# The zeros of an accumulated output: 24 small DMAs in the first stage, or one large DMA behind weight loads

## The chip, the core and the metric

The kernel runs on one core of one Trainium2 chip. The metric is the device time of one execution in microseconds (us). The matrix engine is PE (its weight loads PEld), the vector engine DVE, the scalar engine ACT, GpSimd POOL, and SP is the engine that does nothing but issue DMAs and wait. SP, ACT and POOL each put DMAs into a queue of their own (q1, q10 and q0 in the profile); 16 DMA engines work on all queues.

## The reference

Three layers follow one another on 3072 tokens (4 batches of 768) of 512 values (8 heads of 64):

```
state = gamma * state + k[t] v[t]^T ;  y[t] = scale * q[t] state        # retention, per batch and head
logits = x @ phi ; d = softmax over tokens ; c = softmax over slots     # soft MoE: 8 experts x 4 slots
slots = d.T @ x ; slot_out[e] = relu(slots[e] @ w1[e]) @ w2[e] ; x = c @ slot_out
logits = x @ w_gate + log1p(exp(x @ w_noise)) * noise                   # second MoE: top 2 of 8 experts
out[mask] += weight * (relu(x[mask] @ w1[e]) @ w2[e])                   # for each expert e
```

The last line sums into an output that starts as zeros, and this is where the zeros of this case come from.

## The kernel before

All inputs and the output are float32. The work has three stages, in one program.

*Retention and logits* (lines 203 to 468). A loop over `j` takes 24 chunks of 128 tokens, one ahead in some steps. PE transposes k (`k_t`) and q (`q_t`), multiplies them (`qk`), and forms the output (`y_out`) and the state (`kv`); `x_n` turns the output back. DVE scales the transposed q into `qT` (L267), masks the products into `am` (L287) and scales the result into `xT` (L308). ACT and POOL prepare k and v. For every four chunks, the functions `group0` to `group4` do the softmax of the soft MoE step by step. On SP the loop also issues the loads of q, k and v, and the first MoE's first weights W1 in 28 parts (L456). And it writes the zeros: at L457 to L461, in chunks 1 to 21, DVE makes a zero tile `zt` of 128 x 128 (the bits of `xT`, and-ed with 0, so that it runs no earlier than that chunk) and SP sends it to the output, repeated four times along a row, 256 KB a DMA in pieces of 512 bytes. The tile has two buffers, so that DVE waits before the third for the first one's DMA.

*First MoE's experts and the gate* (lines 469 to 644). `ph` (L516) multiplies the slots with W1, `po` (L549) with W2. W2's parts are loaded by SP into buffers as these come free (`load_w`, L187). At L565 to L567 SP then loads the second MoE's first weights: V1[0], V2[0] and V1[1], 2 MB each, V1[1] into the pool `ringv`. Next come the gate logits, the choice of two experts (DVE, `top`, `cand`, `sel`) and the weights `wsl`. At L639 ACT's queue writes `wsl` into the table `ctab` in memory, two DMAs in which each value row is 8 numbers, 32 bytes, and behind them come three of the four parts of V1[2] (L644).

*Second MoE's experts* (from L647). `lists` finds for each expert the tokens that chose it. `fetch` gathers their rows of `ctab` (L748), so that it needs the writes of L639. `turn` splits and transposes them into `cts`; `hidden` (L801) multiplies with `gs`, the slot outputs already multiplied with V1; `main` (L834 to L836) multiplies with V2, each float32 product as three. `add_rows` (L815) adds the rows to the output in memory, by an indirect DMA of POOL. Before the first expert, ACT casts V2[0] into its high parts (`wh`, L776), splits `g` (L665) and copies it (L681), all in order.

What sets the order around the change: each engine runs its instructions in the order of the program as scheduled, and each waits for its own inputs. SP's order behind the weights of the first experts is: V1[0], V2[0], V1[1], then the copies of `gs` for expert 1 (L687).

Of the kernel before, what the change touches and what calls it, by code (L numbers as in the profile page):

```python
# [9 lines left out]
F32 = mybir.dt.float32  # L10
F32R = mybir.dt.float32r
F16 = mybir.dt.float16
I32 = mybir.dt.int32
AF = mybir.ActivationFunctionType
OP = mybir.AluOpType
# [4 lines left out]
N = B * S  # L20
DM = H * D
P = 128
C = 128
NC = S // C
NCH = B * NC
HP = H // 2
# [10 lines left out]
TL = 64  # L37
LB = SB + 1
WP = 19
ZP = 21  # L40
HV = 7
FB, FN = 7, 6
F1, F2, F3, F4 = 2, 0, 0, 26
# [60 lines left out]
def kernel(ctx: ExitStack, tc: tile.TileContext, q, k, v, phi, w1, w2,  # L104
                              wg, wn, noise, v1, v2, csta, cst, cst16, out):
    nc = tc.nc
# [24 lines left out]
    def after(*ins):  # L131
        stack = ExitStack()
        for i in ins:
            stack.enter_context(tc.issue_after(i.ins if hasattr(i, "ins") else i))
        return stack

    def fill(pool, tag, n, bufs=None):
        if not n:
            return
        pw = pool.tile([P, DM], F32, name="pw", tag=tag, bufs=bufs)  # L140
        for i in range(n):
            nc.tensor.matmul(pw, ones, ones[:, None, :].to_broadcast([P, 4, P]), start=True, stop=True)
# [44 lines left out]
    def load_w(store, src, e, eng, ring, halves=False):  # L187
        t = ring.tile([P, 4096], F32, name="w", tag="w")
        if store is V2:
            nc.sync.dma_start(t.rearrange("p (k n) -> p k n", k=KF), src[e].rearrange("(k p) n -> p k n", p=P))  # L190
            store[e] = t
            return
        s = src[e].rearrange("(p k) n -> p (k n)", p=P)
        if halves:
            tv, sv = (a.rearrange("p (g i n) -> p i g n", g=4, i=2) for a in (t, s))
            for i in range(2):
                eng.dma_start(tv[:, i], sv[:, i])
        else:
            eng.dma_start(t, s)
        store[e] = t  # L200
# [3 lines left out]
    with ExitStack() as actx:  # L204
        work = actx.enter_context(tc.tile_pool(name="work", bufs=2))
        small = actx.enter_context(tc.tile_pool(name="small", bufs=2))
# [6 lines left out]
        def load_q(t):  # L213
            b, u = divmod(t, NC // 2)
            x = comp[:, t % 2]
            nc.sync.dma_start(
                x.rearrange("p h r d -> p h (r d)"),
                q[b, :, 256 * u:256 * u + 256, :].rearrange("h (p r) d -> p h (r d)", r=2))
            QL[t] = x
# [7 lines left out]
        def load_kv(u, gs=range(2)):  # L227
            b, t = divmod(u, NC // 2)
            raw = RAW.setdefault(u, [])
            for i, src in enumerate(() if raw else (k, v)):  # L230
                x = raws[:, 2 * (u % 2) + i]
                nc.sync.dma_start(x.rearrange("p h r d -> p h (r d)"),
                                  src[b, :, 256 * t:256 * t + 256, :].rearrange("h (p r) d -> p h (r d)", r=2))
                raw.append(x)
            for g in gs:
                j = 2 * u + g
                if u % 2:
                    KL[j] = io.tile([P, H, D], F32, name="kl", bufs=2)
                    VL[j] = io.tile([P, H, D], F32, name="vl", bufs=2)
                else:  # L240
                    KL[j], VL[j] = (comp[:, 2 + i].rearrange("p h r d -> p (h r d)")[:, DM * g:DM * g + DM]
                                    .rearrange("p (h d) -> p h d", h=H) for i in range(2))
                gs = slice(64 * g, 64 * g + 64)
                for r in range(2):
                    rs = slice(64 * r, 64 * r + 64)
                    nc.scalar.copy(KL[j][rs], raw[0][gs, :, r, :])
                    pool_ins[0] = nc.gpsimd.tensor_tensor(VL[j][rs], raw[1][gs, :, r, :],  # L247
                                            gv[gs, r, t, :, None].to_broadcast([64, H, D]), op=OP.mult)
# [21 lines left out]
        def k_t(j):  # L270
            pt = psA.tile([P, HP, P], F32, name="pt", tag="pt")
            for hp in range(HP):
                nc.tensor.transpose(pt[:, hp, :], KL[j][:, 2 * hp:2 * hp + 2, :], ident)
            KT[j] = io.tile([P, HP, P], F32, name="kT", bufs=2)
            return nc.scalar.copy(KT[j], pt)  # L275

        def qk(j):
            t, g = divmod(j, 2)
            pa = [psA.tile([P, HP, P], F32, name="pa", tag="pa") for _ in range(2)]
            for hp in range(HP):  # L280
                for s in range(2):
                    r = slice(64 * s, 64 * s + 64)
                    mm = nc.tensor.matmul(pa[s][:, hp, :], KT[j][r, hp, :], QT[t][r, hp, g, :],  # L283
                                          start=True, stop=True)
            for s in range(2):
                a = io.tile([P, HP, P], F32, name="am", bufs=3)
                nc.vector.tensor_tensor(a, pa[s], mask_b, op=OP.mult)  # L287
                AM[j, s] = a
            return mm

        pS = psA.tile([P, HP, D], F32, name="pS", bufs=1)
        X, XT = {}, {}
# [106 lines left out]
            nc.vector.tensor_copy(cT[:, g, :], pc)  # L399

        NT = NCH // 2
        ov = out.rearrange("(p a) d -> p a d", p=P)
        fill(psA, "py", FS)
        load_q(0)
        nc.sync.dma_start(cta, csta)
# [14 lines left out]
        for j in range(NCH + 1):  # L420
            t, g = divmod(j, 2)
            if g == 0 and t and t + 1 < NT:
                load_kv(t + 1)
            if j < NCH:
                if j + 1 < NCH:
                    kt = k_t(j + 1)
                    if j < 1:
                        with after(kt):
                            load_kv(1)
                    if todo:  # L430
                        todo.pop(0)()
                    qk(j + 1)
                tn, s = (t + 1, 1) if g == 0 else (t + 2, 0)
                if tn < NT:
                    q_t(tn, s)
                if todo:
                    todo.pop(0)()
                y_out(j)
                if g == 0 and t + 2 < NT:
                    load_q(t + 2)  # L440
                with after(*([qk0] if j == 0 else [])):
                    kv(j)
            if j:
                if j == NCH:
                    group0(NG - 1)
                x_n(j - 1)
                if j == NCH - 3:
                    load_w(W1, w1, E - 1, nc.sync, ringr)
                if j == NCH - 2:
                    load_w(W2, w2, 0, nc.sync, ringb)  # L450
                for i in range(28 * (j - 1) // WP, 28 * j // WP if j <= WP else 0):
                    if i % 4 == 0:
                        W1[i // 4] = (ringp if i < 8 else ringa).tile([P, 4096], F32, name="w", tag="w")
                    s = slice(1024 * (i % 4), 1024 * (i % 4) + 1024)
                    nc.vector.tensor_copy(W1[i // 4][0:1, s][:, 0:1], XT[j - 1][0:1, 0, 0:1])
                    nc.sync.dma_start(W1[i // 4][:, s], w1[i // 4].rearrange("(p k) n -> p (k n)", p=P)[:, s])  # L456
                for i in range(NCH * (j - 1) // ZP, NCH * j // ZP if j <= ZP else 0):  # L457
                    zt = small.tile([P, P], I32, name="zt")
                    nc.vector.tensor_single_scalar(zt, XT[j - 1][:, 0, :].bitcast(I32), 0, op=OP.bitwise_and)
                    nc.sync.dma_start(ov[:, i, :].rearrange("p (a d) -> p a d", d=P),  # L460
                                      zt.bitcast(F32)[:, None, :].to_broadcast([P, HP, P]))  # L461
                if j == 8:
                    with after(pool_ins[0]):
                        load_small()
                if j % 4 == 0:
                    gi = j // 4 - 1
                    todo += [lambda f=f, gi=gi: f(gi) for f in (group0, group1, group2, group3, group4)]
# [60 lines left out]
    with rctx, bctx:  # L528
        ringd = bctx.enter_context(tc.tile_pool(name="ringd", bufs=1, reuse_waits="tile"))
        small = bctx.enter_context(tc.tile_pool(name="smallb", bufs=1, reuse_waits="tile"))  # L530
# [33 lines left out]
        ringv = rctx.enter_context(tc.tile_pool(name="ringv", bufs=1, side="right", reuse_waits="tile"))  # L564
        load_w(V1, v1, 0, nc.sync, ringa)  # L565
        load_w(V2, v2, 0, nc.sync, ringb)
        load_w(V1, v1, 1, nc.sync, ringv)  # L567
        small = rctx.enter_context(tc.tile_pool(name="rt", bufs=1, side="right", reuse_waits="tile"))
        psw = psB.tile([P, 2 * E], F32, name="psw", tag="pm", bufs=1)
        for kd in range(KD):  # L570
# [366 lines left out]
    with tc.If(most > SB * P + TL):  # L937
        with tc.tile_pool(name="ov", bufs=1) as ov_p, tc.tile_pool(name="ovr", bufs=1) as ring, tc.tile_pool(name="ovp", bufs=1, space=PSUM) as ov_s:
            for e in range(E):
# [16 lines left out]
                with tc.For_i(SB, nc.values_load(ci[:, e:e + 1], min_val=0, max_val=NB)) as ib:  # L956
# [15 lines left out]
                    for kf in range(KF):  # L972
# [5 lines left out]
                        out=out, out_offset=bass.IndirectOffsetOnAxis(ap=idx[:, :1], axis=0),  # L978
# [30 lines left out]
```

## Time and profile before

| | us |
|---|---|
| Runs of the kernel (3) | 605.96, 606.19, 609.58; median 606.19 |
| Profiled execution | 603.33 |
| its span, first to last instruction | 601.5 |
| PE busy in the span | 562.4 |

A row of the page or of a view names the line, the engine and the operation, then output<-input tiles. A time in a timeline is counted from the span's start. Where a row says `[0.97 <-DVE qT L267]`, the engine sat idle 0.97 us before it, until that instruction of another engine was done.

### The profile page before, as it was taken

To read this page: it belongs to the slowest core of one execution; us is meant where nothing else is said; L and a number is where in the kernel's file an instruction comes from. 1 tells how busy PE (TensorE), PEld (TensorE's weight loads), DVE (VectorE), ACT (ScalarE), POOL (GpSimd) and SP (SyncE) were. 2 spreads that over 40 slices of the span, in tenths; PEclk is the share of its full clock that TensorE was granted. 3 is DMA by queue.
4 is the path that set the end of the run, shared out by engine and by line. 5 is a ranking of instruction groups with operands and counts; after the bars stand their busy time and mean duration, and the time that the engine had idled before them with its cause. 6 is when DMAs were issued, how large, how long until landed. Compare 5 with 4: busy or idle time off the path is not lost. (4 is left out here: it accounts for less than half of the span.)

```text
span 601.5 us, 11094 instructions
## 1 busy us (share of the span) xinstructions
PE 562.4 (94%) x4296; PEld 431.3 (72%) x4296; DVE 268.0 (45%) x606; ACT 243.2 (40%) x536; POOL 229.1 (38%) x231
## 2 busy tenths in 40 slices
PE   6999899999999888999999999999999999999990
PEld 3887677878653445788787787787887887788880
DVE  3766686776410076465335145245245235234200
ACT  2564455554300044455336246246246245334200
POOL 2543543341211026545445345345344445232231
PEclk8999999999979995999999999999999999999996
DMA  9999999988789963367556556566566554453241
GB/s 247 268 320 328 279 318 277 300 265 280 272 314 417 405 200 116 62 177 197 113 108 181 107 143 183 108 147 178 114 142 176 115 129 68 114 113 47 37 54 20
DMA packets 88065, 111.80 MB, mean 186 GB/s; under 512 B 10482, under 2 KB 64306, under 8 KB 86722
## 3 DMA queue, kind: packets, MB, share of 16 engines
q1 hardware_dynamic: 73840, 94.75, 48.7%
q0 software_dynamic: 9952, 14.37, 16.9%
q10 hardware_dynamic: 4210, 1.87, 1.3%
q8 instruction: 36, 0.59, 0.4%
q14 instruction: 27, 0.22, 0.1%
HBM read 87.92 MB, written 20.41 MB: 180 GB/s over the span
## 5 line engine op out<-in xcount | busy, mean ns | idle before, releaser
L834 PE MATMUL pyc<-wh,hhl 128*128 128x512 f32 x384 | 153.9, 401 | 0.0
L815 POOL DMA_INDIRECT out_dram<-yo,ls x56 | 88.9, 1588 | 165.9 <-ACT hhl L804 34.5
L835 PE MATMUL pyc<-wl,hhl 128*128 128x512 f32 x384 | 151.5, 394 | 0.0
L836 PE MATMUL pyc<-wh,hhl 128*128 128x512 f32 x384 | 151.3, 394 | 0.0
L806 DVE SCALAR_TENSOR_TENSOR hhl<-phc,hhl 128x512 fp32r<-128x512 f32 (+1 forms) x128 | 66.7, 550 | 72.7 <-ACT hhl L804 72.3
L836 PEld LDWEIGHTS pyc<-wh,hhl 128*128 128x128 f32 x384 | 72.4, 189 | 16.3
L834 PEld LDWEIGHTS pyc<-wh,hhl 128*128 128x128 f32 x384 | 72.7, 189 | 15.2 <-issue 0.4
L843 ACT ACTIVATE yo<-pyc,cg 128x512 f32<-128x512 f32 x48 | 33.0, 688 | 124.4 <-PE pyc L836 115.6
L835 PEld LDWEIGHTS pyc<-wl,hhl 128*128 128x128 f32 x384 | 72.5, 189 | 14.4
L748 POOL DMA_INDIRECT cg<-ctab,ls x56 | 57.0, 1018 | 27.8 <-issue 16.6
L782 DVE TENSOR_TENSOR wl<-w,wh 128x1024 fp32r<-128x1024 f32 x32 | 39.1, 1225 | 56.7 <-ACT wh L776 56.7
L804 ACT ACTIVATE hhl<-phc 128x512 fp32r<-128x512 f32 (+1 forms) x128 | 59.4, 514 | 11.7 <-PE phc L801 10.4
L776 ACT CAST wh<-w 128x1024 fp32r<-128x1024 f32 x32 | 33.5, 1049 | 33.0 <-DMA w<-in_moe_w_dram 25.2
L247 POOL TENSOR_TENSOR comp<-raws,cta 64x512 f32<-64x512 f32 x24 | 24.9, 1038 | 46.4 <-PE pS L316 13.4
L287 DVE TENSOR_TENSOR am<-pa,cta 128x512 f32<-128x512 f32 x48 | 32.4, 688 | 17.5 <-PE pa L283 14.5
L801 PE MATMUL phc<-cts,gs 128*128 128x256 f32 (+1 forms) x192 | 37.3, 304 | 0.5 <-ACT cts L770 0.5
L267 DVE TENSOR_TENSOR qT<-pt,cta 64x512 f32<-64x512 f32 x48 | 33.0, 688 | 10.2 <-PE py L301 4.7
L801 PEld LDWEIGHTS phc<-cts,gs 128*128 128x128 f32 x192 | 29.9, 195 | 6.8 <-issue 2.1
L247 POOL TENSOR_TENSOR vl<-raws,cta 64x512 f32<-64x512 f32 x24 | 24.9, 1038 | 25.8 <-PE pS L316 13.1
L321 ACT COPY sbd<-pS 64x256 f32<-64x256 f32 x40 | 14.7, 366 | 46.3 <-PE pS L316 45.8
L283 PE MATMUL pa<-qT,kT 64*128 64x128 f32 x384 | 28.8, 291 | 2.0 <-ACT kT L275 2.0
L283 PEld LDWEIGHTS pa<-qT,kT 64*128 64x128 f32 x384 | 24.1, 193 | 8.8 <-ACT kT L275 6.9
(177 smaller groups left out, 730.3 us busy)
## 6 DMA issues: line engine op xcount, KB each, us to landing
w<-in_moe_w_dram SPq DMA_DIRECT2D x77, 512.0 KB, 5.0
w<-in_moe_w_dram SPq DMA_DIRECT2D x11, 2048.0 KB, 16.2
comp<-in_q_dram SPq DMA_DIRECT2D x12, 512.0 KB, 8.6
raws<-in_k_dram SPq DMA_DIRECT2D x12, 512.0 KB, 8.4
raws<-in_v_dram SPq DMA_DIRECT2D x12, 512.0 KB, 8.1
out_dram<-zt SPq DMA_DIRECT2D x24, 256.0 KB, 6.7
gs<-gr SPq DMA_DIRECT2D x112, 32.0 KB, 2.5
w<-in_moe_w_dram SPq DMA_DIRECT2D x2, 1024.0 KB
```

The costliest lines, as they stand in the source:

```text
L247: pool_ins[0] = nc.gpsimd.tensor_tensor(VL[j][rs], raw[1][gs, :, r, :], gv[gs, r, t, :, None].to_broadcast([64, H, D]), op=OP.mult)
L283: mm = nc.tensor.matmul(pa[s][:, hp, :], KT[j][r, hp, :], QT[t][r, hp, g, :], start=True, stop=True)
L748: nc.gpsimd.indirect_dma_start(out=cg[:rows(b), i, :], out_offset=None, in_=ctab, in_offset=index(e, b, rows(b)))
L776: ins = nc.scalar.copy(wh, V2[e][:, 1024 * i:1024 * i + 1024])
L782: nc.vector.tensor_tensor(wl, V2[e][:, 1024 * i:1024 * i + 1024], WH[e][i], op=OP.subtract)
L801: nc.tensor.matmul(ph[:, w * i:w * i + w], GS[e][:, kf + i], CT[e, g][:, :w], start=True, stop=True)
L804: relu.append(nc.scalar.activation(h[:, :, :w], pv, AF.Relu))
L806: last = nc.vector.scalar_tensor_tensor(h[:, :, w + t0:w + t0 + 2 * P], pv[:, :, :2 * P], 0.0, h[:, :, :2 * P], op0=OP.max, op1=OP.subtract)
L815: nc.gpsimd.indirect_dma_start(out=out, out_offset=index(e, b, n), in_=y, in_offset=None, bounds_check=N - 1, oob_is_err=False, compute_op ...
L834: nc.tensor.matmul(py, hhl[:, kf, ts], wh, start=(kf == 0), stop=False)
L835: nc.tensor.matmul(py, hhl[:, kf, ts], wl, start=False, stop=False)
L836: nc.tensor.matmul(py, hhl[:, kf, tl], wh, start=False, stop=(kf == KF - 1))
```

## The change

The zero tiles and their DMAs leave the retention's loop. Instead, behind the load of V1[1], POOL clears one tile of 128 x 2048 values in the same pool `ringv`, and SP sends it to the output in one DMA: each of the 128 partitions writes its 24 rows of the output, 48 KB in memory in one piece, as six copies of its 8 KB. The whole output is 6.29 MB (3072 x 512 x 4 bytes), by both ways.

```diff
-ZP = 21
+ZW = 4 * DM
...
-        ov = out.rearrange("(p a) d -> p a d", p=P)
...
-                for i in range(NCH * (j - 1) // ZP, NCH * j // ZP if j <= ZP else 0):
-                    zt = small.tile([P, P], I32, name="zt")
-                    nc.vector.tensor_single_scalar(zt, XT[j - 1][:, 0, :].bitcast(I32), 0, op=OP.bitwise_and)
-                    nc.sync.dma_start(ov[:, i, :].rearrange("p (a d) -> p a d", d=P),
-                                      zt.bitcast(F32)[:, None, :].to_broadcast([P, HP, P]))
...
         load_w(V2, v2, 0, nc.sync, ringb)
         load_w(V1, v1, 1, nc.sync, ringv)
+        zt = ringv.tile([P, ZW], F32, name="zt")
+        nc.gpsimd.memset(zt, 0.0)
+        nc.sync.dma_start(out.rearrange("(p a) d -> p (a d)", p=P).rearrange("p (a d) -> p a d", d=ZW),
+                          zt[:, None, :].to_broadcast([P, N * DM // (P * ZW), ZW]))
```

## Rows read from the trace of the kernel before

**Rows 1.** The profile's page: the span, the engines' busy time, PE's clock in 40 slices.
```profile
span 601.5 us, 11094 instructions
...
PE 562.4 (94%) x4296; PEld 431.3 (72%) x4296; DVE 268.0 (45%) x606; ACT 243.2 (40%) x536; POOL 229.1 (38%) x231
...
PEclk8999999999979995999999999999999999999996
```

**Rows 2.** Windows (columns: PE, PEld, DVE, ACT, POOL busy, clock, DMA share, GB/s).
```profile
226.00:241.00 15.00, 13.33 (x64) 8.20 (x63) 9.23 (x14) 7.21 (x19) 9.54 (x12) 0.56 0.36 106
241.00:590.00 349.00, 345.70 (x1839) 276.91 (x1837) 135.57 (x303) 146.14 (x326) 148.29 (x124) 1.00 0.53 121
```

**Rows 3.** Windows, the retention from 20 to 160 us.
```profile
20.00:160.00 140.00, 129.46 (x1672) 107.24 (x1669) 98.71 (x225) 71.66 (x159) 52.89 (x57) 1.00 0.95 288
```

**Rows 4.** Waits of PE, 20 to 160 us: the two largest of five.
```profile
PE pd L362 <- ACT dT L354: 4.9, 5, 1.2
PE pt L273 <- DVE qT L267: 3.5, 4, 1.7
```

**Rows 5.** Groups by line, and the tile `zt` (min/median/max ns): DVE's zero tiles.
```profile
L459 DVE TENSOR_SCALAR zt<-xT 128x128 int32<-128x128 int32 x24 | 10.7, 444 | 6.8 <-DMA out_dram<-zt 6.8
...
L459 DVE TENSOR_SCALAR zt<-xT x24: 204/228/1086, 22.3 to 146.9; 128x128 int32<-128x128 int32 x24
```

**Rows 6.** DMA issues: the zeros.
```profile
out_dram<-zt SPq DMA_DIRECT2D x24, 256.0 KB, 6.7
```

**Rows 7.** Timeline of DVE and PE, at two late zero tiles.
```profile
60.59 0.23 DVE L459 TENSOR_SCALAR zt<-xT 128x128 int32<-128x128 int32 x1 [2.89 <-DMA out_dram<-zt]
...
62.86 0.63 PE L273 MATMUL pt<-ct,comp 128*128 128x128 f32 x4 [1.70 <-DVE qT L267]
...
104.00 0.23 DVE L459 TENSOR_SCALAR zt<-xT 128x128 int32<-128x128 int32 x1 [1.55 <-DMA out_dram<-zt]
...
108.96 0.63 PE L273 MATMUL pt<-ct,comp 128*128 128x128 f32 x4 [0.97 <-DVE qT L267]
```

**Rows 8.** Groups by line: POOL's memset of `siT`; and a wait of POOL, 196 to 260.
```profile
L503 POOL MEMSET siT<- 128x1152 f32 x1 | 1.1, 1056 | 0.0
...
POOL w L629 <- DVE top L600: 17.0, 1, 17.0
```

**Rows 9.** Timeline of SP: the load of V1[1] and what SP issues next.
```profile
195.00 7.19 SPq L199 DMA_DIRECT2D w<-in_moe_w_dram  x1
226.80 1.99 SPq L687 DMA_DIRECT2D gs<-gr  x3
```

**Rows 10.** Tile `out_dram`: the accumulating writes (min/median/max ns, first and last start).
```profile
L815 POOL DMA_INDIRECT out_dram<-yo,ls x56: 1419/1572/2082, 251.8 to 588.0; - x56
```

**Rows 11.** DMA queues (packets, MB, share of 16 engines): 180 to 190, then 215 to 220.
```profile
q1 hardware_dynamic: 292, 4.21, 99.2%
...
q1 hardware_dynamic: 26, 0.16, 7.9%
```

**Rows 12.** Timeline of ACT and PE, 219 to 234.
```profile
219.34 1.55 ACTq L639 DMA_DIRECT2D ctab<-wsl  x2
...
222.78 1.99 ACT L776 CAST wh<-w 128x1024 fp32r<-128x1024 f32 x2 [0.27 <-issue]
...
229.78 1.20 ACT L681 CAST gs<-gw 128x256 fp32r<-128x256 f32 x4 [2.06 <-PE gw L679]
230.87 0.25 ACT L760 CAST cts<-cg 128x64 fp32r<-128x64 f32 x1
...
233.89 1.65 PE L801 MATMUL phc<-cts,gs 128*128 128x256 f32 x6 [0.46 <-ACT cts L770]
```

**Rows 13.** DMA queues, 220.6 to 222.6: the writes into the table.
```profile
q10 hardware_dynamic: 3107, 0.11, 76.4%
```

**Rows 14.** DMA queues, 6.5 to 7.0: two queues at once.
```profile
q1 hardware_dynamic: 204, 0.10, 85.8%
q10 hardware_dynamic: 199, 0.03, 41.5%
```

## The prediction

> **What bounds the kernel now.** I read the profile's page first, then windows, waits and timelines of the stages that the change touches. It shows a span of 601.5 us in which PE is busy for 94%, at full clock but for a few dips [rows 1]. Cut into stretches, the two parts differ. From 241 to 590 us PE is busy for 345.7 of 349.0 us at clock 1.00 [rows 2]: this part (the second MoE's experts) has no slack, so whatever delays its start delays the end by the same amount, and nothing later gives it back. The stretch before it, 226 to 241, has PE at a mean clock of 0.56 and no steady work [rows 2]: here a chain of small steps decides. The first part, the retention, is the one that loses work. From 20 to 160 us PE is busy for 129.5 of 140 us, the DMA engines for 95% [rows 3]. Of PE's 10.5 idle us, 4.9 end with ACT's exponential (five times, once per group of chunks) and 3.5 with DVE's qT (four times) [rows 4]; no wait of PE ends with a DMA. So the full DMA engines do not set the pace there; PE does, and DVE now and then.
>
> The trace's own execution took 603.33 us (span 601.5), the median of the runs is 606.19. I make the sum against 603.33 and add the difference, 2.9 us, at the end.
>
> **What is removed.** In the retention 24 DVE instructions go; they are 10.7 us busy and wait 6.8 us for earlier zero DMAs to free one of two small tiles [rows 5]. With them go 24 issues of SP and 24 DMAs of 256 KB [rows 6]. What of it lies on PE's path? The timeline shows the mechanism twice: DVE stands 2.89 us before a zero tile, its next qT comes late, and PE's transposes then wait 1.70 us for qT; the same with 1.55 us and 0.97 us [rows 7]. I credit all four such waits, 3.5 us [rows 4], though only these two are surely the tile's. In each of the five groups one zero tile (0.23 us in the median [rows 5]) stands in DVE's short chain between the maximum and the exponential that PE waits for: 5 x 0.2 = 1.0 us. Sum: 4.5 us gained. The bounds: nothing (PE's next wait, for ACT's kT, takes over; or below it by 1 us, if the instructions fall into a worse order), and all of DVE's time, 10.7 + 6.8 = 17.5 us, if DVE paced every chunk. I stay near the low end, since PE is the one without gaps. What PE saves here reaches the next stage whole: W2's loads go into buffers that W1 and the retention leave, so they move with PE.
>
> **What is added, and hidden.** A GpSimd memset of 128 x 2048 values: the one of 128 x 1152 took 1.06 us [rows 8], so about 1.9 us, on POOL, which waits 17.0 us for DVE's top values at about that time [rows 8]. SP's issue of one DMA: it comes right behind the first experts' last load, whose issue began at 195.00 and held SP for 7.19 us; SP's next instruction is at 226.80 [rows 9]. Both cost nothing. The copies issued there, for expert 1, now queue behind the zeros; an expert takes some 44 us (349 us by 8), so they are needed 40 us later. The accumulating writes to the output, which must wait for the zeros, first start at 251.8 [rows 10]. If the zeros end by 232, that wait has 18 us of cover.
>
> **What is moved: 6.29 MB onto the DMA engines at a bad place.** Loads in 16 KB packets move 4.21 MB in 10 us with the engines 99.2% busy [rows 11]: 26.5 GB/s an engine, so 0.31 us for 8 KB and 14.8 us for the zeros' 48 packets on each of 16 engines. Those loads are through a little after 215 (0.16 MB is left from there on [rows 11]). So the zeros would hold all engines from about 215.5 to 230 to 232. In the trace of before these engines are free then, and that matters: at 219.34 ACT issues two DMAs that put the gate weights into the table which the gathers read, then three loads of V1[2] [rows 12]. The put is 3072 packets of 32 bytes, 192 an engine; alone they went through in 2.0 us, by 222.6 [rows 13].
>
> How do two queues share an engine? The trace has one clean case: from 6.5 to 7.0 us ACT's queue (q10) with 128-byte packets ran beside SP's (q1) with 512-byte packets, and 199 packets of the one went with 204 of the other [rows 14]. They take turns packet by packet, whatever their size. So a put packet would wait for an 8 KB packet each time, 0.31 us. From 220.6 to 231.5 some 35 of the 192 get through; the other 157 follow when the zeros are out: 157/192 x 2.0 = 1.6 us. The put ends at 232 to 234 instead of 222.6: 9.4 to 11.4 us later, I take 10.4.
>
> What stands behind it? A DMA issue lasts until its queue has room: SP's of one 2 MB load took 7.19 us behind two others [rows 9]. ACT would so stand in its issues until about 233, and all that ACT does next (the casts of the first weights at 222.78, the copy of g at 229.78, cts at 230.87 [rows 12]) shifts. The gathers need the put as well, and PE's first g of expert 2 needs V1[2]. The first hidden product, PE at 233.89 [rows 12], comes 10.4 us later, and from there PE is the bound. PE idles longer before it. [...]
>
> Sum: -4.5 + 10.4 + 0.5 = +6.4 us. 603.3 + 6.4 = 609.7, and with the 2.9 us to the median 612.6.
>
> The bounds of the move: 0, if the put slips through at once; and some 25 us (10.4 + 14.8), if writes of 8 KB went at half the loads' rate. No row shows a write of that size; the nearest are the loads of 16 KB, whose rate I use.
>
> **Rivals.**
>
> *Several put packets at a turn.* If an engine took about ten of the 32-byte packets for each zero packet, the put would need 19 turns of 0.31 us, 5.9 us where it took 2.0: 3.9 us late, and the loads behind it a little more; I take 5. Sum -4.5 + 5 + 0.5 = +1, 607 us. For it: a run of so small packets could be fetched together. Against it: the records count 3107 packets in those 2 us, each value its own [rows 13], and the turns at 6.5 us were one to one. [...]
>
> *The put is not held.* The zeros are hidden wholly in the idle DMA time from 215 to 232, as the windows there suggest at first sight (7.9% busy from 215 to 220 [rows 11]). Then only the gain is left, with 1 us for crowding: -3.5, 602.7 us, faster than before though within 1%. Against it are rows 14.
>
> *DVE paces the retention.* Its 98.7 us of 140 [rows 3], in order, feed three of PE's steps. If 10 to 17 us of the 17.5 came back, 14 in the middle, the sum is -14 + 10.9 = -3, 603 us, also not slower. Against it: PE's gaps add up to 10.5 us in all.
>
> *Slow writes.* 8 KB writes at half rate: +6.4 + 14.8 = +21, 627 us. Nothing in the rows speaks for it; 512-byte zeros beside loads landed in 6.7 us like their neighbours [rows 6].
>
> **How the numbers follow.** Forecast 0.58, by itself 607 to 619; several at a turn 0.14; not held 0.12; DVE paces 0.10; slow writes 0.06. A measurement of this kernel tells about 1%, 6 us, from no change. The forecast's middle lies at that border: of its 0.58 some 0.34 are beyond +6 us and 0.24 within. With slow writes (0.06) and a little of the second (0.03) slower gets 0.43. Faster by over 1% needs a gain of 10 us or more with little delay: about a quarter each of not held and DVE paces, and a remainder for what I do not see, 0.11. The rest, 0.46, is within 1%. The range, 602 to 621, leaves out slow writes and the better half of the two fast cases.
>
> **What would show it.** Right: no zero tiles on DVE and PE's retention some 4 us shorter, the hidden stage's first product at about 240 instead of 233.9; 768 packets of 8 KB from about 212 to 232 on SP's queue with few 32-byte packets among them; ACT's issue of the put's loads stretched by 10 us; PE from there on as before, busy nearly throughout. Wrong: the table's 32-byte packets through within 3 us beside the zeros, or a retention shorter by more than 9 us, or zero packets much longer than 0.31 us.

## The result, and the profile after

| | before | after |
|---|---|---|
| Median, same chip (20 runs each) | 607.16 us (604.74 to 610.90) | 610.25 us (608.67 to 619.52) |
| Ratio after/before | | 1.0068, 95% interval 1.0048 to 1.0088 |
| Profiled execution, its span | 603.33, 601.5 us | 610.11, 608.3 us |

The change costs 0.7% by the ratio, some 4 us (the medians differ by 3.1 us): clearly slower, though by less than 1%. The ratio leaves out one slow run of the changed kernel, the one of 619.52 us. The page of the changed kernel answers to [rows 1]: DVE is 7.7 us less busy, PE nearly unchanged, but spread over a longer span; the lowest digit of the clock's row, a 5, stands in the same slice as before.

```profile
span 608.3 us, 11028 instructions
...
PE 561.6 (92%) x4296; PEld 428.8 (71%) x4296; DVE 260.3 (43%) x582; ACT 243.2 (40%) x536; POOL 232.2 (38%) x232
...
PEclk9999999999999785999999999999999999999997
```

Windows (columns as in [rows 2]) of the changed kernel: the retention, the stretch before the second MoE, and the main part.

```profile
20.00:160.00 140.00, 131.45 (x1697) 108.41 (x1697) 91.09 (x204) 72.60 (x160) 54.91 (x58) 1.00 0.83 249
...
226.00:241.00 15.00, 9.61 (x67) 4.27 (x67) 5.95 (x8) 6.74 (x14) 6.50 (x6) 0.50 0.53 154
241.00:590.00 349.00, 346.36 (x1843) 276.79 (x1843) 140.35 (x310) 148.98 (x335) 149.59 (x128) 1.00 0.53 123
```

PE works 2.0 us more within the same 140 us of the retention [rows 3] and as densely as before from 241 to 590 [rows 2]. In between it loses: 3.7 us less work from 226 to 241, with the clock at 0.50 throughout.

PE's waits from 20 to 160 us show where the retention's gain came from. The wait for DVE's qT fell from 3.5 to 1.3 us, the wait for ACT's exponential did not move [rows 4].

```profile
PE pd L362 <- ACT dT L354: 4.9, 5, 1.2
PE pt L273 <- DVE qT L267: 1.3, 3, 0.7
```

What follows was late all the same. ACT's timeline answers to [rows 12]:

```profile
217.07 10.04 ACTq L637 DMA_DIRECT2D ctab<-wsl  x2
227.20 2.92 ACTq L642 DMA_DIRECT2D w<-in_moe_w_dram  x2
...
230.65 1.99 ACT L774 CAST wh<-w 128x1024 fp32r<-128x1024 f32 x2 [0.27 <-issue]
...
237.65 1.20 ACT L679 CAST gs<-gw 128x256 fp32r<-128x256 f32 x4 [2.05 <-PE gw L677]
238.71 0.28 ACT L758 CAST cts<-cg 128x64 fp32r<-128x64 f32 x1
```

The put is issued 2.3 us earlier than before (217.07 against 219.34) but takes 10.04 us to issue instead of 1.55. The first cast comes 7.9 us later than before, at 230.65. PE shows the same delay. Its first hidden product starts at 241.89, 8.0 us later than in [rows 12]:

```profile
230.52 1.62 PE L709 MATMUL pli<-bt,oh 128*128 128x14 f16 x24 [10.77 <-ACT cnt L624]
...
241.89 0.98 PE L799 MATMUL phc<-cts,gs 128*128 128x256 f32 x6 [0.60 <-ACT cts L768]
```

PE stood for 10.77 us until ACT, out of its DMA issues, had copied the counts (`cnt`). The DMA engines say what ACT stood for. Queues (packets, MB, share of 16 engines), first 221 to 226 us, then 227 to 230 us:

```profile
q1 hardware_dynamic: 256, 2.10, 99.0%
q10 hardware_dynamic: 248, 0.01, 2.8%
```
```profile
q10 hardware_dynamic: 2711, 0.09, 47.5%
q1 hardware_dynamic: 27, 0.14, 11.2%
```

In those 5 us 256 packets of 8 KB and 248 of 32 bytes went: one for one. An engine so passed 15.5 put packets in 5 us, 0.32 us each. Counts over 5 us would also come out so if both queues went in bundles of equal number. A stretch as long as one turn, from 222 to 222.32 us, tells these apart: 16 of each kind on the 16 engines.

```profile
q1 hardware_dynamic: 16, 0.13, 96.9%
q10 hardware_dynamic: 16, 0.00, 2.8%
```

When the zeros were nearly out, 2711 of the put's 3072 packets went in 3 us (227 to 230).

Between 242 and the end two more things move. The first add's scaling (`yo`) starts at 254.15 against 248.26 in the kernel before, only 5.9 us later, and that of the fifth at 286.37 against 278.50, 7.9 later:

```profile
254.15 0.69 ACT L841 ACTIVATE yo<-pyc,cg 128x512 f32<-128x512 f32 x1 [1.01 <-issue]
...
286.37 0.69 ACT L841 ACTIVATE yo<-pyc,cg 128x512 f32<-128x512 f32 x1 [3.85 <-PE pyc L834]
...
595.14 0.69 ACT L841 ACTIVATE yo<-pyc,cg 128x512 f32<-128x512 f32 x1 [4.86 <-PEq L935]
```
```profile
248.26 0.69 ACT L843 ACTIVATE yo<-pyc,cg 128x512 f32<-128x512 f32 x1 [1.19 <-PE pyc L836]
...
278.50 0.69 ACT L843 ACTIVATE yo<-pyc,cg 128x512 f32<-128x512 f32 x1 [3.85 <-PE pyc L836]
...
586.97 0.69 ACT L843 ACTIVATE yo<-pyc,cg 128x512 f32<-128x512 f32 x1 [4.86 <-PEq L937]
```

The first fence is the changed kernel, the second the kernel before. Up to the first `yo` PE ran 72 products here and 80 before, so part of the 2.1 us is only another order. From the first hidden product to the fifth `yo` both kernels run 235 products. These are the windows of that stretch (columns as in [rows 2]), first the kernel before, then the changed one:

```profile
233.89:278.50 44.61, 44.43 (x235) 35.78 (x236) 25.22 (x69) 19.62 (x52) 24.28 (x26) 0.94 0.52 133
241.89:286.37 44.48, 42.43 (x235) 33.64 (x236) 25.43 (x69) 19.50 (x52) 24.40 (x26) 1.00 0.52 136
```

The same products keep PE busy 2.0 us less, and this is the clock: it is full here throughout (1.00), where before PE restarted while the clock was still at 0.50 (0.94 in the mean; the first six products take 0.98 us here and 1.65 in [rows 12]). PE idles 1.9 us more: 1.0 us for ACT's hhl, 0.8 for POOL's bt and 0.2 for hhl, where before it idled 0.2 us in all. The last `yo` is 8.2 us late and the tail behind it 1.4 us shorter. So, between the two profiles: -2.3 (put issued earlier) +10.3 (from the put to the first hidden product, 24.8 us instead of 14.55) -2.0 +1.9 +0.3 -1.4 = +6.8.

### The profile page after: what moved, and what is told of

It is laid out like the page before. It is cut to its first block, busy times and chain, and to the rows that moved or that the text cites. A ratio compares the mean times of both kernels' runs of the same rounds, so it can differ in the third digit from the quotient of the medians.

```text
span 608.3 us, 11028 instructions
## 1 busy us (share of the span) xinstructions
PE 561.6 (92%) x4296; PEld 428.8 (71%) x4296; DVE 260.3 (43%) x582; ACT 243.2 (40%) x536; POOL 232.2 (38%) x232
## 5 line engine op out<-in xcount | busy, mean ns | idle before, releaser
L802 ACT ACTIVATE hhl<-phc 128x512 fp32r<-128x512 f32 (+1 forms) x128 | 59.2, 514 | 10.3 <-PE phc L799 7.4
```

Source lines behind the costliest of these rows:

```text
L802: relu.append(nc.scalar.activation(h[:, :, :w], pv, AF.Relu))
```

## The experiments

My theory: the loss is the put, held by turns with the zeros' packets, and ACT standing in its issue; the gain is the zero tiles' waits in the retention. The rivals: the zeros cost where they are for another reason (order on SP, DMA bandwidth), or the gain is the DMA engines' relief. Each experiment was timed beside the kernel before on the same chip; its median there varied from 605.05 to 607.62 us between the sets, so I compare ratios.

**No zeros.** The zeros are written nowhere; the program is otherwise the changed one.

```diff
-        zt = ringv.tile([P, ZW], F32, name="zt")
-        nc.gpsimd.memset(zt, 0.0)
-        nc.sync.dma_start(out..., zt...)
```

> Left out: the output's zeros are written nowhere, neither in the retention nor behind V1[1]; the rest is the changed kernel. Theory (the zeros hold the table's 32-byte packets, and ACT behind them): the retention stays as in the changed kernel (hidden product of the soft MoE at about 167.2 instead of 169.9), the two writes into the table are issued in under 2 us and through by about 221, and the second MoE's first hidden product comes at about 231 (233.9 before, 241.9 changed). Time 2 to 4 us under the kernel before, ratio 0.994 to 0.997. Rival (the loss comes from the changed order of instructions or another memory layout, not from the zeros' transfer): first hidden product still at 238 or later, time 2 to 5 us above the kernel before.

Measured: 601.61 us, ratio 0.9934 (0.9906 to 0.9962). ACT and PE in the timeline of this run:

```profile
214.64 1.55 ACTq L633 DMA_DIRECT2D ctab<-wsl  x2
...
218.07 1.99 ACT L770 CAST wh<-w 128x1024 fp32r<-128x1024 f32 x2 [0.27 <-issue]
...
229.88 0.98 PE L795 MATMUL phc<-cts,gs 128*128 128x256 f32 x6 [1.21 <-ACT cts L764]
```

The put issues in 1.55 us and the first hidden product comes 15.2 us behind it, not 24.8. By the ratios the retention's relief is worth 0.66% (4.0 us), and the zeros in their new place cost 1.0068/0.9934 = 1.35% (8.2 us); the intervals leave each some 2 us either way.

**Half the zeros.** Three of six packets a partition; half of the output's zeros are written nowhere.

```diff
-                          zt[:, None, :].to_broadcast([P, N * DM // (P * ZW), ZW]))
+                          zt[:, None, :].to_broadcast([P, 3, ZW]))
```

> The changed kernel with half of its zeros: 3 of the 6 packets of 8 KB a partition, 24 on each of 16 engines; the other half of the output's zeros is written nowhere. Theory (the loss is the time that the put's packets spend taking turns with zero packets): the zeros end about 7.4 us earlier, near 220.5 by the changed kernel's clock, only some 10 of an engine's 192 put packets are held, ACT's first put issue or its first load issue is 3 to 4 us long instead of 10.04, the put is through by about 223, first hidden product 233 to 235 (where e1_no_zeros has 229.9 and the changed kernel 241.9), 603 to 605 us. Rival (any zeros there cost the same, by the reuse of buffers or by the order on SP): first hidden product near 241, 609 to 610 us.

Measured: 603.86 us, ratio 0.9973 (0.9949 to 0.9996). Timeline of ACT and PE:

```profile
216.69 2.26 ACTq L638 DMA_DIRECT2D ctab<-wsl  x2
219.04 3.35 ACTq L643 DMA_DIRECT2D w<-in_moe_w_dram  x2
...
222.91 1.99 ACT L775 CAST wh<-w 128x1024 fp32r<-128x1024 f32 x2 [0.27 <-issue]
...
234.02 1.65 PE L800 MATMUL phc<-cts,gs 128*128 128x256 f32 x6 [0.46 <-ACT cts L769]
```

From put to first hidden product it takes 17.3 us: 2.1 more than without zeros, where all the zeros cost 9.6 more. So the cost is not that of having such a DMA there, nor of SP's order, nor even in proportion to bytes. What fits both runs is the time for which the zeros outlast the put's issue.

**Small zero packets.** The same DMA in 512-byte packets.

```diff
-ZW = 4 * DM
+ZW = P
```

> The zeros stay behind V1[1] in one DMA, but from a tile of 128 values, so in packets of 512 bytes (12288 of them, 768 an engine). Theory (queues take turns packet by packet): a 512-byte packet takes about 0.03 us, so 192 turns take 6 to 7 us: the table's packets are through at 224 to 226, although the zeros last longer than in the changed kernel (until about 235); ACT's issue of them takes 4 to 6 us instead of 10; first hidden product at 236 to 238, time 605 to 608. Rival (what counts is the zeros' bytes or their time on the engines: the table's packets wait until the zeros are out): packets through after 235, first hidden product at 247 or later, time 613 to 616.

Measured: 612.73 us, ratio 1.0120 (1.0080 to 1.0161); the first hidden product at 242.25. Queues of this run from 222 to 230 us, and ACT's timeline:

```profile
q1 hardware_dynamic: 3569, 1.83, 86.8%
q10 hardware_dynamic: 2844, 0.09, 18.9%
```
```profile
218.14 4.42 ACTq L637 DMA_DIRECT2D ctab<-wsl  x2
222.66 6.00 ACTq L642 DMA_DIRECT2D w<-in_moe_w_dram  x2
...
228.78 2.33 ACTq L642 DMA_DIRECT2D w<-in_moe_w_dram  x1
231.15 1.99 ACT L774 CAST wh<-w 128x1024 fp32r<-128x1024 f32 x2 [2.24 <-issue]
```

The turns get shorter: with packets a sixteenth as long an engine passes 178 put packets in 8 us beside 223 of the zeros', 0.045 us each instead of 0.32, and the put goes through while the zeros still run (1035 packets on SP's queue from 230 to 236 us). But the time was 5 us above what I expected. I had reckoned with some 0.03 us a turn and the put through by 226; at 230 us, 228 of its 3072 packets had still to go. ACT stands 4.42 us in the put's issue. It stands another 6.00 and 2.33 us in the issues of V1[2]'s loads, although up to 230 us only put packets went on its queue (2844 packets are 0.09 MB, 32 bytes each). So it was still the put that held ACT, and the casts are as late as in the changed kernel. The smaller packets shorten a turn, but now all of the put's packets go beside zeros, where in the changed kernel most went when the zeros were nearly out.

**The put on POOL's queue.** POOL issues the put, ACT only the loads.

```diff
-            put = nc.scalar.dma_start(row_view(r)[:, :, NS:], wsl[64 * r:64 * r + 64])
+            put = nc.gpsimd.dma_start(row_view(r)[:, :, NS:], wsl[64 * r:64 * r + 64])
...
-        with after(put):
+        with after(wexp):    # wexp: the activation (Exp) on w
```

> The changed kernel with the two writes into the table issued by POOL (queue q0) instead of ACT; V1[2]'s three loads stay on ACT's queue, behind the exponential. Theory: the records of q0 put many rows into one packet (a gather of 128 rows is 16 packets), so the table's writes need few turns beside the zeros and land within 4 to 6 us; ACT is not held in its issues and casts the first weights before 222; V1[2]'s 24 packets an engine take turns with 8 KB packets, 0.47 us each, 11 us, until about 228. First hidden product at 232 to 236, time 602 to 606. Rival (any transfer waits until the zeros are out, whatever its queue and packets): table through after 228, first hidden product at 238 or later, time 608 to 611.

Measured: 606.06 us, ratio 0.9990 (0.9958 to 1.0022). ACT, POOL and PE in its timeline:

```profile
217.04 1.04 ACT L774 CAST wh<-w 128x1024 fp32r<-128x1024 f32 x1 [1.37 <-DVE sel L602]
...
232.06 1.06 POOL L746 DMA_INDIRECT cg<-ctab,ls  x1 [8.49 <-issue]
...
236.92 0.24 ACT L758 CAST cts<-cg 128x64 fp32r<-128x64 f32 x1 [7.79 <-DMA cg<-ctab,ls]
...
238.62 1.65 PE L799 MATMUL phc<-cts,gs 128*128 128x256 f32 x6 [0.46 <-issue]
```

This parts the two ways in which the held put hurts. ACT is free at 217.04 and casts at once; now the gathers are late, since they need the table: POOL issues the first at 232.06, and ACT waits 7.79 us for it. So the table was not there within the 4 to 6 us that I expected, and the first hidden product, at 238.62, is later than the 232 to 236 us expected. Freeing ACT is worth 0.8% against the changed kernel. The 0.6% that are left to the run without zeros go with the data's own lateness; no run takes these apart further.

**Zeros behind everything.** 2 KB packets on SP, behind the last load of V1[2]; a one-element POOL instruction on the tile, reading the first gather, holds them.

```diff
-        nc.sync.dma_start(out..., zt...)            # behind V1[1]
+            nc.gpsimd.tensor_tensor(zt[0:1, 0:1], cg0[0:1, 0, 0:1], cg0[0:1, 0, 0:1], op=OP.subtract)
+            nc.sync.dma_start(out..., zt...)        # behind V1[2]
```

> The zeros as one DMA of 2 KB packets still later: behind V1[2]'s last quarter, held until the first gather has landed by a one-element operation on POOL. Theory: the table's writes and V1[2]'s first loads then run alone, first hidden product at about 231; zeros from about 234 to 251; the gathers beside them are a few packets each and lose under 1 us; the first accumulating write waits until about 253, within its three buffers. Time 2 to 4 us under the kernel before, ratio 0.994 to 0.997. Rival (6.3 MB cost their time wherever they stand near the second MoE's start): PE waits for late gathers, weights or buffers between 240 and 270, time 607 or more.

Measured: 614.33 us, ratio 1.0131 (1.0088 to 1.0174). The first half came true: the first hidden product is at 231.93. But the zeros fill the engines from 237 to 254 us. Tile `out_dram`, then the waits of ACT and of PE from 245 to 590 us:

```profile
L811 POOL DMA_INDIRECT out_dram<-yo,ls x56: 1420/1571/2482, 258.9 to 598.1; - x56
```
```profile
ACT yo L839 <- DMA out_dram<-yo,ls: 38.0, 12, 5.9
```
```profile
PE phc L797 <- DVE gr L662: 3.7, 3, 2.1
PE phc L797 <- ACT hhl L800: 2.7, 1, 2.7
```

The first `yo` was ready at 246.33, the first add ran at 258.9. The adds follow one another, 56 of them over 339 us, and hardly go faster than PE makes rows, so the backlog of 12 us shrinks slowly: ACT's last wait for it ends at 457 us. It comes back through the `yo` buffers: ACT waits 38.0 us for adds to free one (0 in the kernel before), what ACT does next is late, and PE, which had been ahead, waits 6.4 us and works 5.2 us more than in the changed kernel, mostly at a clock below full (0.91 from 300 to 340 us). This path is read from the waits; no run tests it by itself.

**Zeros behind the put, on ACT's own queue.** The zeros stand behind the put on one queue, so they should not take turns with it.

```diff
-        nc.sync.dma_start(out..., zt...)
...
+        with after(v12):                            # the third load of V1[2]
+            nc.scalar.dma_start(out..., zt...)      # 4 KB packets
```

> The changed kernel with the zeros issued by ACT behind the put and the first three loads of V1[2] on ACT's own queue, as 1536 packets of 4 KB. Theory (the loss is the put held by turns with the zeros): the put issues in 1.55 us each as in e1_no_zeros, the casts at about 219, first hidden product 230 to 232, zeros out by 242, so before the first add, which comes at about 247; 602 to 604 us, below both kernels. Rival (zeros anywhere in this stretch cost what they take from the gathers, copies and loads beside them, as e4_zeros_late suggests): the first hidden product as early, but late gathers or adds behind it, 606 us or more.

Measured: 609.75 us, ratio 1.0028 (0.9999 to 1.0058). The rival's time came true, and not the theory's 602 to 604 us; the first hidden product came at 234.35, not at 230 to 232. Timeline of ACT, then ACT's waits from 245 to 590 us:

```profile
216.46 1.55 ACTq L635 DMA_DIRECT2D ctab<-wsl  x2
...
220.54 1.99 ACT L775 CAST wh<-w 128x1024 fp32r<-128x1024 f32 x2 [0.92 <-issue]
...
232.42 0.24 ACT L759 CAST cts<-cg 128x64 fp32r<-128x64 f32 x1 [4.54 <-DMA cg<-ctab,ls]
```
```profile
ACT yo L842 <- DMA out_dram<-yo,ls: 7.9, 2, 3.9
```

The put is no longer held (its issue took 1.55 us), but the gathers are slow beside the zeros (ACT waits 4.54 us), and later the adds fall behind and ACT waits 7.9 us for them. Each of the places tried in this stretch has a small transfer that is waited for.

**Where the retention's gain is.** Three edits of the kernel before. First, one constant zero tile, cleared once by POOL; the 24 DMAs stay in their places on SP. Second, the same with a tile of 256 columns, so 1 KB packets. Third, the DVE tiles stay and their DMAs go; there the zeros are written nowhere.

```diff
+        zt = small.tile([P, 128], F32, name="zt", bufs=1)     # 256 in the second
+        nc.gpsimd.memset(zt, 0.0)
...
-                    zt = small.tile([P, P], I32, name="zt")
-                    nc.vector.tensor_single_scalar(zt, XT[j - 1][:, 0, :].bitcast(I32), 0, op=OP.bitwise_and)
+                    with after(*wl[-1:]):                     # the latest W1 load
                         nc.sync.dma_start(ov[:, i, :]..., zt...)
```

> The kernel before, with one constant zero tile set once by POOL in place of the 24 DVE zero tiles; the 24 DMAs of 512-byte packets stay in the retention. Theory (the retention's gain is DVE's zero tiles and their waits): PE waits for qT about 1.3 us instead of 3.5 between 20 and 160 us, ph (L510 of the changed kernel's numbering) at about 167, the put short, first hidden product about 231, 604 us, some 2.7 below the kernel before. Rival (the gain is the DMA engines' relief): the retention as before, ph at about 170, 606.8 us.

> As e5_zero_tile_once, with a zero tile of 1 KB a partition, so 12288 packets of 1 KB in place of 24576 of 512 bytes. [...] If the DMA engines' load plays a part in the retention, this is faster than e5_zero_tile_once by up to 2 us (602 to 603); if not, the same, 604.

> The kernel before with the 24 DVE zero tiles kept and their 24 DMAs left out (the zeros are written nowhere). Theory (the waits of a tile for the DMA that frees it, and not the 10.7 us of DVE's work, are most of the gain): PE's waits for qT fall as in the changed kernel, ph at 167 to 168, 604 to 605 us. Rival (DVE's work itself): ph stays at about 169.5, 606 us or more.

Measured: 603.98 us, ratio 0.9919 (0.9889 to 0.9948); 603.13, 0.9931 (0.9897 to 0.9965); 602.01, 0.9899 (0.9859 to 0.9939). Window 20 to 160 and PE's wait of the third, which keeps all of DVE's work, and of the 1 KB variant, which keeps all the bytes:

```profile
20.00:160.00 140.00, 131.58 (x1697) 108.41 (x1697) 99.63 (x228) 72.57 (x162) 54.67 (x58) 1.00 0.82 249
```
```profile
PE pt L273 <- DVE qT L267: 1.3, 3, 0.7
```
```profile
20.00:160.00 140.00, 131.45 (x1699) 108.40 (x1698) 91.08 (x202) 72.60 (x161) 55.08 (x58) 1.00 0.95 293
```
```profile
PE pt L273 <- DVE qT L267: 1.3, 3, 0.7
```

DVE is as busy as before in the third (99.63 us [rows 3]), the DMA engines as busy as before in the other (0.95), and PE runs the retention equally well in both. So neither DVE's 10.7 us of work nor the engines' load shows a cost in these two; what did was that DVE stood in line for a zero tile that its DMA still held [rows 5, 7]. The single profile of the 512-byte variant is of its slowest execution (609.58 us; the ten others took 601.26 to 605.20) and still shows 2.5 us for qT, where 1.3 was expected. I draw nothing from it, and 512 bytes against 1 KB stays undecided: the 2 us expected of it are an estimate, and the runs show 6144 packets fewer on SP's queue (67696 against 73840) at the same DMA share from 20 to 160 us, 0.95 against 0.95 in the kernel before [rows 3]. Both write all the zeros and beat both kernels, by some 0.7 to 0.8% against the kernel before and 1.4% against the changed one.

## Why the prediction was right, and where it was off

The forecast was 612.6 us against a profile of 603.33 (+6.4) and 2.9 more to the median. Measured were +6.8 between the profiles and +0.7%, 4 us, between the runs. The difference to the median counts twice there: the changed kernel's own profile, 610.11, lies at its median, and that of before, 603.33, below all 20 of its runs. That +6.8 is so near to +6.4 is luck in part. In the profile the retention gave 2.3 us (the earlier put) and not 4.5; the clock gave back 2.0 where I had put a loss of 0.5; and two terms that I had not foreseen, PE's new waits and the shorter tail, came to +0.8 together with the 0.3 us that was left over. By the runs the gain is 4.0 and the cost 8.2, not 10.9.

- *What bounds it.* Right for this change: from the first hidden product on, the delay reaches the end (8.0 us there, 8.2 at the last `yo`), though on the way it was 5.9. As a rule it is too strong. Without zeros the first hidden product came 12.0 us earlier than in the changed kernel, and the span was only 8.6 us shorter (599.7 against 608.3 us): there PE slowed down once more, its 128x512 products taking 0.63 us from 240.55 to 244.85, as in the kernel before at a clock of 0.50, and 0.39 from 246.10. With the zeros behind everything it came 10 us earlier, and the time was longer.
- *The zero tiles, 3.5 us of qT waits.* Right mechanism; in the profile 2.2 of the 3.5 went, and 1.3 us have another cause. The step "one zero tile in DVE's short chain, 5 x 0.2 = 1.0 us" was wrong: the wait it names is 4.9 us in every kernel, and with the tiles kept and only their DMAs gone the gain is the same. What the runs put in its place: 4.0 us in all by the ratio, of which the profiles show 2.7 (`ph` from 169.87 to 167.18 us). A part of that difference is scatter: with the same retention program `ph` started at 165.51 without zeros and at 168.53 with the put on POOL.
- *Hidden additions.* Right: POOL's memset took 1.80 us, SP's issue 0.62, and no wait of PE names either.
- *The turns.* Right, nearly to the number: one for one, 0.32 us a turn, 0.309 us an 8 KB packet (256 in 99.0% of the 16 engines' 5 us); with 512-byte packets 0.045 us a turn, though 223 of the zeros' packets went there with 178 of the put's. With the put on POOL's queue the zeros and ACT's loads went one for one as well, 230 and 228 packets from 222 to 230 us (1.88 and 0.80 MB). Each 32-byte value had its own turn (16 beside 16 packets in 0.32 us), and the rival "several put packets at a turn" falls. Were both queues to go in bundles of equal number, the counts of 5 us would come out so too, and so would [rows 14]; the 0.32 us would not.
- *The put 10.4 us late, ACT with it.* Right: from the put's issue to the first cast 13.6 us instead of 3.4, so 10.1 us. The length of ACT's issues went with the packets still queued: the put's took 1.55 us with free engines, 2.26 with half the zeros and 10.04 here (364 of its 3072 packets had gone by 227 us), and the loads' behind it took 6.00 and 2.33 us with the 512-byte zeros.
- *The clock, +0.5.* Wrong in sign: -2.0 us. No run shows the 0.5 us of the sum. What the runs showed in its place: the clock was 0.50 from 226 to 241 us and 0.89 from 241 to 242, where before it was 0.50 from 226 to 239 and 0.84 from 239 to 240. So the stretch at 0.50 did end later. But PE's restart, at 241.89, now came behind that stretch and not inside it, so that it ran at a clock of 1.00. The length of the pause does not decide this in the runs: without zeros the first six products, at 229.88, took 0.98 us behind a longest wait of 1.61 us since 215 (10.77 here), and with the put on POOL's queue, at 238.62, they took 1.65 behind one of 3.48. This is the term that was mis-sized; with the new short waits (+1.9) and the shorter tail (-1.4) it makes up the sum in the profile.
- *The rivals.* "The put is not held" falls to the no-zeros run, 1.35% faster. "DVE paces the retention" falls to the run that keeps all of DVE's work. "Slow writes" falls to 0.309 us an 8 KB packet.

Not settled: why the runs of one kernel scatter as they do (the kernel before from 601.34 to 611.87 us over the sets, the changed one from 608.67 to 619.52), and where in the profile the rest of the 4.0 us of gain lies.

## What to carry to other kernels

A DMA moved to where the DMA engines look idle must be held against every small transfer that starts there: turns went packet by packet here, so large packets on one queue multiply the time of many tiny ones on another (0.32 us each beside 8 KB, where 192 an engine took 2.0 us alone), and the engine that issues the tiny ones stops computing (10.04 us in one pair of issues). Ask also which buffer ties a cheap instruction to a DMA; here a constant source tile, with the DMAs left in place, takes the gain without the loss. And the first write that must wait for the moved one can be the real end of the slack: adds that hardly outrun PE work off a late start slowly (here 12 us took some 200).

## What the runs showed that was not expected

- A put of 3072 packets of 32 bytes keeps its issuing engine: ACT stood 10.04 us in an issue that takes 1.55 with free DMA engines, 2.26 with half the zeros.
- With half the zeros the put still ran beside their last packets, yet its cost was 2.1 of 9.6 us at half the bytes: here the cost went with the overlap in time and not with the bytes.
- A delay of PE's restart gave some of itself back: the restart at 241.89 us came behind the stretch at a clock of 0.50, and the same 235 products kept PE busy 42.43 us instead of 44.43.
- ACT came out of its DMA issues only when the put's packets were nearly out, with 8 KB zeros as with 512-byte ones: with the latter it stood 4.42, 6.00 and 2.33 us in them, 12.8 us in all, almost as long as in the changed kernel.
